# Causal window attention and soft experts: 64-query strips, token-major values with row sums, one VectorE step for bias and maximum

## The chip, the cores and the metric

The kernel runs on one core of one Trainium2 chip. The metric is the device time of one execution in microseconds; a profiled execution gives a span, from the first to the last instruction, and the trace behind the lines below. The five engines are TensorE (PE, with PEld for its weight loads), VectorE (DVE), ScalarE (ACT), GpSimd (POOL) and SyncE (SP, which issues most DMAs).

## The reference

Attention with a causal window of 128 keys and a linear bias by distance, over 8 batches, 8 heads, 576 tokens, 64 features a head; then a mixture of soft experts (8 experts with 4 slots each, so 32 slots) over all 4608 tokens:

```python
scores = q @ k.T / sqrt(64) - slope[h] * abs(i - j)   # only 0 <= i - j < 128
attn = softmax(scores) ; x = attn @ v                 # (B, H, S, D)
x = x.transpose(0, 2, 1, 3).reshape(4608, 512)
logits = x @ phi                                      # (4608, 32)
d = softmax(logits, over tokens) ; c = softmax(logits, over slots)
slot_in = d.T @ x                                     # (32, 512)
slot_out[e] = relu(slot_in[e] @ w1[e]) @ w2[e]        # 512 -> 1024 -> 512
return c @ slot_out                                   # (4608, 512)
```

All of it is in float32.

## The kernel before, in words

**Attention loop.** A batch has five query tiles: four of 128 queries and a tail of 64. A full tile is done in two groups of four heads; the tail is one group of eight heads. This makes 9 groups a batch and 72 in all. A group always holds 4 x 128 columns of scores on 128 partitions (queries on the partitions). The order on each engine is written out by hand (`manual_schedule`), and the loop over `i` walks the groups in a pipeline: group i gets its softmax, group i-3 is transposed, group i-4 meets the values, group i+1 gets its scores.

One group's steps, with the lines of the profile:

- `scores`: TensorE first writes the distance bias into PSUM (bf16 products of `ones` and `ramp`, L248, or L236 for a batch's first tile) and adds the products of 32-query strips with 160 keys (L255, L241). Two halves of the array's rows (two heads) and four column groups (four strips) work at once.
- `merge` (VectorE, L270; L268 and L272 in first and tail tiles): the window of a query covers 128 of the columns held; a predicated copy folds the two triangles into one 128 x 128 square.
- `rowmax` (L290) and `bias` (L293, maximum times the scale), VectorE.
- `expo` (ScalarE, L342): four exponentials of 128 columns, each with its row sum read out (ACTIVATION_READ_ACCUMULATOR).
- `total` (POOL, L298), `inverse` (L302) and `normalise` (L307, four multiplications), VectorE: the probabilities are divided by the row sum.
- `flip` (L352): four transposes; `split`: a copy to SBUF by ScalarE (L359) and two `affine_select` by POOL (L361, L363) that take the folded square apart into the keys of this tile and of the one before.
- `values` (L388): per head, v is the stationary operand (64 columns) and 128 queries stream; x comes out with the features on the partitions. `x_store` (L404, ScalarE) copies it, `x_flip` (L409) and `x_keep` (L418) make the token-major copy.

**Slots, once a batch.** `logits` (L427) for the tiles of the batch, a running maximum and sum over the tokens, transposes, `slot_sum` (L510) and `slot_add` (L523) with rescaling, and the softmax over the slots (L534 to L547) in gaps of VectorE (`fillers`).

**Weights.** w1 and w2 make 64 units of 512 KB. `load_weights_at` spreads the first `NW` = 36 over the loop; 11 more go into buffers that attention has no more use for (`place`), the last 17 into ring buffers that the experts free.

**End.** After the loop stands a hand-written chain for the last groups. Then the experts: `hidden` (L911), `expert_out` (L947), `slot_stack`, `combine` (L968, L974) in the order of `TAIL_ORDER`; `turn` transposes the combine weights.

Of the kernel before, what the change touches and what calls it, by code (L numbers as in the profile page):

```python
# [25 lines left out]
NT = 5  # L26
# [5 lines left out]
NTT = 36  # L32
UW = 1024
NW = 36
KB = 32
WIN = P + KB
NB = S // KB
HW = 512
CW = P + TAIL + NS
WARM = 6  # L40
WEND = 66
W0 = 10
EAGER = 2
FLAG = 3
LAG = 4
FINAL = (3, 4, 0)
# [6 lines left out]
TAIL_ORDER = '''s0 b0v b1a b2v e1n e13 k0 e12 c00 e15 c01 e16 s1 c02 e2n e24 k1 e22 c10 e25 c11 e25 s2 c12 e3n e34 k2 e32 c20 e35 c21 e35 s3 c22 k3 c30 c31 c32'''  # L53
# [3 lines left out]
def width(t):  # L57
    return P if t < 4 else TAIL
# [10 lines left out]
def tile_attn_softmoe(  # L69
# [4 lines left out]
    vd: bass.AP,  # L74
    phid: bass.AP,
    w1d: bass.AP,
    w2d: bass.AP,
    slopes: bass.AP,
# [11 lines left out]
    mask_u = cst[:, 0:P].bitcast(I32)  # L90
    mask_t = cst[:, P:P + TAIL].bitcast(I32)
    delta = cst[:, P + TAIL:]
    pick, sel = cst[:, 0:P], cst[:, P:P + 2 * NS]
    unit_r = cpool.tile([P, P], F32R, name="unit_r")
    ident = unit_r.bitcast(F32)
    fine = cpool.tile([P, 14], F32, name="fine")
    low, m_run, s_run = fine[:, 0:1], fine[:, 1:3], fine[:, 3:4]
    comb = cpool.tile([P, NS], F32, name="comb")
    mix = cpool.tile([P, NS], F32, name="mix")
# [4 lines left out]
    kq = cpool.tile([P, 3 * UW], F32, name="kq")  # L104
    ramp = cpool.tile([P, 2, 2, WIN], BF16, name="ramp")
    ones = cpool.tile([P, P], BF16, name="ones")
    area = cpool.tile([P, 19, HW], F32, name="area")

    kall = kq[:, 0:NB * P].rearrange("p (n j w) -> p n j w", n=NB, j=NPAIR)
    qs = [kq[:, NB * P + 2 * P * i:NB * P + 2 * P * i + 2 * P] for i in range(3)]  # L110
    half = [slice(64 * par, 64 * par + 64) for par in range(2)]

    def halves(i):
        return area[:, i].rearrange("p (u w) -> p u w", u=4)

    xts = [halves(i) for i in (0, 1, 12, 13)]
    xt_t = halves(17)
    p4s = [halves(i) for i in (2, 3, 18)]
    pas, pps = [halves(i) for i in (6, 8, 7)], [halves(i) for i in (7, 9)]
    vs = [area[:, i] for i in (11, 5, 10)]  # L120
    xns = [area[:, i] for i in (16, 4, 14, 15)]
# [3 lines left out]
    areas = {i: area[:, i:i + 2].rearrange("p a w -> p (a w)") for i in range(0, 18, 2)}  # L125
    place = [ks[1], areas[14], ks[0], ks[2]] + [areas[i] for i in (0, 10, 6, 4, 16, 12, 8)]
# [3 lines left out]
    def load_weight():  # L130
# [12 lines left out]
    def order(b):  # L143
        return (1, 2, 3, 4, 0) if b == last else range(NT)

    def pos(b, t):
        return order(b).index(t)

    def lane(b, t):
        return (t - 1) % 4 if b == last else t  # L150

    groups = [(b, t, g) for b in range(B) for t in order(b) for g in range(2 if t < 4 else 1)]
    number = {key: i for i, key in enumerate(groups)}
    n = len(groups)
    v_loads = [(b, t) for b in range(B) for t in range(NT)]
    fin = slice(3 * NS, P)
# [7 lines left out]
    def load_q(i, eng=None):  # L164
        b, t, g = groups[i]
        o = 4 * P * t + 2 * P * g
        (eng or nc.sync).dma_start(qs[i % 3], qd[b, :, o:o + 2 * P])

    def load_k(b, t, eng=None):
        o, e = 4 * P * t, min(4 * P * (t + 1), NB * P)  # L170
        (eng or nc.sync).dma_start(kq[:, o:e], kd[b, :, o:e])

    v_slot = {}

    def load_v(again=False):
        if again:
            b, t, v_slot[last, 0] = last, 0, area[:, 13]
        else:
            b, t = v_loads[len(v_taken)]
            v_slot[b, t] = vs[len(v_taken) % 3]  # L180
            v_taken.append((b, t))
        nc.sync.dma_start(v_slot[b, t][0:width(t)], vd[b, P * t:P * t + width(t)])

    def load_v_pair():
        new = [len(v_taken), len(v_taken) + 1]
        for i in new:
            v_slot[v_loads[i]] = vs[i % 3]
            v_taken.append(v_loads[i])
        for o in (0, DM // 2):
            for i in new:  # L190
                b, t = v_loads[i]
                nc.sync.dma_start(
                    v_slot[b, t][:, o:o + DM // 2], vd[b, P * t:P * t + P, o:o + DM // 2])

    v_taken = []

    with tc.manual_schedule(engines=ORDERED):
        warm = area[:, 2].bitcast(BF16)[:, 0:512]
        nc.vector.memset(warm, 0.0)
        nc.vector.memset(low, LOW)  # L200
        nc.vector.memset(ramp, 0.0)
        nc.vector.memset(ones, 1.0)
        nc.vector.memset(fine[:, 10:11], -1.0)
        nc.gpsimd.memset(cst[:, 0:P], 1.0)
        nc.gpsimd.affine_select(cst[:, 0:P], cst[:, 0:P], [[1, P]], ALU.is_gt, 0.0, base=0, channel_multiplier=-1)
        load_k(0, 0)
        load_q(0, nc.scalar)
        for par in range(2):
            nc.sync.dma_start(ramp[64 * par:64 * par + 1], slopes[par:par + 1])
        load_q(1, nc.scalar)  # L210
        load_q(2, nc.scalar)
        load_k(0, 1)
        tiny = work.tile([P, 1], F32, tag="nm", name="tiny")
# [3 lines left out]
        nc.gpsimd.memset(lg, LOW)  # L217
        nc.gpsimd.memset(area[:, 3, 0:P], 1.0)
        nc.gpsimd.affine_select(
            unit_r, area[:, 3, 0:P], [[1, P]], ALU.is_equal, 0.0, base=0, channel_multiplier=-1)  # L220
        load_v()
        nc.scalar.dma_start(cst[:, P:], cstd)
        nc.scalar.dma_start(phi, phid)
        for t in range(2, NT):
            load_k(0, t)

    def scores(i):
        b, t, g = groups[i]
        s4 = s4s[i % 2]
        parts = [s4[:, 0:2], s4[:, 2:4]]  # L230
        if i == 0:
            parts = [ps_1.tile([P, 2, 2 * P], F32, tag=tag, name="s4_0") for tag in ("pt", "xp")]
        qt = qs[i % 3].rearrange("p (j w) -> p j w", w=width(t))
        if t == 0:
            for par, rows in enumerate(half):
                nc.tensor.matmul(  # L236
                    parts[par][:, :, 0:P], lhsT=ones[rows], rhs=ramp[rows, g, :, 0:P],
                    start=True, stop=False)
            for jj in range(2):
                for par, rows in enumerate(half):  # L240
                    nc.tensor.matmul(  # L241
                        parts[par][:, jj, 0:P], lhsT=qt[rows, jj], rhs=kall[rows, 0:4, 2 * g + jj],
                        start=False, stop=(jj == 1))
        else:
            strips = [(c // 2, c % 2) if t == 4 else (g, c) for c in range(4)]
            for par, rows in enumerate(half):
                for c, (h, r) in enumerate(strips):
                    nc.tensor.matmul(  # L248
# [848 lines left out]
```

## Time and profile before

| what | value |
|---|---|
| time, median of 3 runs | 290.92 us (289.94 to 291.21) |
| span of the profiled execution | 289.1 us; of its time outside the span nothing is recorded |
| busy PE / DVE / ACT / POOL | 272.9 / 233.3 / 204.5 / 92.7 us |
| mean granted TensorE clock | 0.980 |
| last scores of the loop begin | 216.28 us |
| the experts' first product begins | 235.74 us |
| DMA | 72.58 MB, mean 251 GB/s |

Busy time is the union of an engine's records. A TensorE record is a latency (270 to 300 ns for a product), and records overlap, so a busy TensorE may still take more work; the distance between starts tells what one product costs. DMA share is the mean busy share of the core's 16 DMA engines. A group's line in the page gives the line of code, the engine, what is written and read, the count, then busy time, the mean of one, and the idle time before it with what ended it.

### The profile page before, as it was taken

What the parts mean: (1) busy time and instruction counts of PE and PEld (TensorE: products, weight loads), DVE (VectorE), ACT (ScalarE), POOL (GpSimd) and SP (SyncE); (2) the same over time, 40 slices, a digit from 0 to 9 for tenths busy, and PEclk for the clock granted to TensorE, in tenths of its full rate; (3) what the DMA queues carried; (4) which work ended last, traced back from release to release, by engine and by line L of the source; (5) the groups of instructions that cost most, each with busy time, mean ns of one, the idle gap of its engine ahead of it and who ended that gap; (6) DMA issues with size and microseconds to landing.
All of it is one profiled execution on the core that took longest, in us unless ns stands there. A gap on an engine that the chain in (4) does not pass through costs nothing.

```text
span 289.1 us, 13085 instructions
## 1 busy us (share of the span) xinstructions
PE 272.9 (94%) x5164; PEld 191.0 (66%) x5164; DVE 233.3 (81%) x729; ACT 204.5 (71%) x811; POOL 92.7 (32%) x206
## 2 busy tenths in 40 slices
PE   7499999999999999999999999999899999999983
PEld 3367777777677767776777677767676753476641
DVE  3899999999989999988999999979989443234452
ACT  2788888978988978978798887978797241023351
POOL 2025515442444354235324550634455001000000
PEclk9799999999999999999999999999999999999995
DMA  6645278868786887867678869675547789999897
GB/s 193 223 131 169 81 228 266 261 201 284 212 265 201 287 279 242 246 231 247 216 249 258 282 199 291 218 252 173 185 158 238 231 285 311 417 417 398 352 378 285
DMA packets 35025, 72.58 MB, mean 251 GB/s; under 512 B 4210, under 2 KB 15124, under 8 KB 34964
## 3 DMA queue, kind: packets, MB, share of 16 engines
q1 hardware_dynamic: 34244, 71.24, 74.0%
q8 instruction: 41, 0.67, 0.9%
q10 hardware_dynamic: 720, 0.51, 0.6%
q14 instruction: 20, 0.16, 0.1%
HBM read 62.29 MB, written 9.44 MB: 248 GB/s over the span
## 4 chain that ended last, share of the span: by engine, by line
PE 47%; DVE 44%; ACT 3%; issue 3%; POOL 1%; ACTq 0%; DVEq 0%; POOLq 0%
DVE area L307 16%; DVE s L290 11%; PE xp L388 8%; DVE s L270 6%; PE op L947 5%; PE hp L911 5%; PE po L968 4%; PE pt L352 4%; PE s L255 4%; DVE s L268 3%; PE xq L409 2%; PE lp L427 2%; ACT area L342 2%; PE s L248 2%; PE ap L510 1%
## 5 line engine op out<-in xcount | busy, mean ns | idle before, releaser
L342 ACT ACTIVATE area<-s,nb 128x128 f32<-128x128 f32 x288 | 102.5, 374 | 21.5 <-DVE nb L293 20.2
L307 DVE TENSOR_SCALAR area<-area,rs 128x128 f32<-128x128 f32 x286 | 79.2, 338 | 0.6 <-DVE nb L293 0.3
L388 PE MATMUL xp<-area 128*64 128x128 f32 (+1 forms) x1104 | 75.2, 271 | 2.2 <-POOL area L361 1.3
L388 PEld LDWEIGHTS xp<-area 128*64 128x64 f32 x1104 | 56.2, 136 | 17.4 <-issue 8.7
L342 ACT ACTIVATION_READ_ACCUMULATOR area<-s,nb 128x1 f32 x288 | 60.8, 211 | 0.0
L290 DVE TENSOR_REDUCE s<-s 128x4 f32<-128x512 f32 x71 | 49.5, 698 | 2.2
L359 ACT COPY area<-pt 128x512 f32<-128x512 f32 x70 | 42.0, 600 | 11.0 <-PE pt L352 10.8
L298 POOL TENSOR_SCALAR rs<-sm 128x4 f32<-128x4 f32 x70 | 13.8, 197 | 99.7 <-ACT area L342 98.9
L352 PE MATMUL pt<-unit_r,area 128*128 128x128 f32 x284 | 45.6, 282 | 0.0
L255 PE MATMUL s<-kq 64*32 64x160 f32 x1792 | 42.0, 302 | 0.3 <-DMA kq<-k_t 0.3
L352 PEld LDWEIGHTS pt<-unit_r,area 128*128 128x128 f32 x284 | 31.9, 142 | 14.2 <-PE s L255 5.0
L361 POOL TENSOR_SCALAR_AFFINE_SELECT area<-area 128x512 f32<-128x512 f32 x48 | 31.6, 658 | 25.8 <-ACT area L359 24.5
L270 DVE COPY_PREDICATED s<-cst,s 128x512 f32<-128x512 int32 x48 | 32.9, 686 | 0.7 <-PE s L255 0.5
L363 POOL TENSOR_SCALAR_AFFINE_SELECT area<-area 128x512 f32<-128x512 f32 x48 | 31.4, 655 | 3.3
L255 PEld LDWEIGHTS s<-kq 64*32 64x32 f32 x1792 | 29.6, 107 | 1.0 <-DMA kq<-q_t 0.5
L248 PE MATMUL s<-ramp,ones 64*32 64x320 bf16 x448 | 18.7, 310 | 5.0 <-ACT area L342 4.8
L974 DVE COPY ob<-po 128x384 f32<-128x384 f32 x24 | 12.5, 554 | 13.5 <-PE po L968 11.8
L409 PE MATMUL xq<-unit_r,area 128*128 128x128 f32 x136 | 22.0, 284 | 0.5
L404 ACT COPY area<-xp 128x512 f32<-128x512 f32 (+1 forms) x37 | 20.9, 565 | 2.0 <-PE xp L388 1.6
L418 ACT COPY area<-xq 128x512 f32<-128x512 f32 x34 | 20.8, 611 | 0.0
L974 ACT COPY ob<-po 128x384 f32<-128x384 f32 x24 | 10.5, 482 | 13.7 <-PE po L968 13.7
L409 PEld LDWEIGHTS xq<-unit_r,area 128*128 128x128 f32 x136 | 14.5, 141 | 6.4 <-issue 3.2
(167 smaller groups left out, 309.8 us busy)
## 6 DMA issues: line engine op xcount, KB each, us to landing
w<-w SPq DMA_DIRECT2D x53, 512.0 KB, 5.1
out<-ob SPq DMA_DIRECT2D x24, 384.0 KB, 4.2
kq<-q_t SPq DMA_DIRECT2D x69, 128.0 KB, 3.2
kq<-k_t SPq DMA_DIRECT2D x32, 256.0 KB, 3.7
area<-v_n SPq DMA_DIRECT2D x31, 256.0 KB, 4.3
area<-w SPq DMA_DIRECT2D x8, 512.0 KB, 5.0
area<-v_n SPq DMA_DIRECT2D x12, 128.0 KB, 3.4
kq<-w SPq DMA_DIRECT2D x3, 512.0 KB, 6.3
```

What stands on the lines that cost most here:

```text
L248: nc.tensor.matmul(s4[32 * c:32 * c + 32, 2 * par:2 * par + 2, 32 * r:32 * r + WIN], lhsT=ones[rows, 0:32], rhs=ramp[rows, h], start=True, ...
L255: nc.tensor.matmul(s4[32 * c:32 * c + 32, 2 * par + jj, 32 * r:32 * r + WIN], lhsT=qt[rows, 2 * h + jj if t == 4 else jj, 32 * r:32 * r + 32],
L270: nc.vector.copy_predicated(s4[:, :, P:2 * P], bc(mask_u, 1, 4), s4[:, :, 0:P])
L290: nc.vector.tensor_reduce(st[key]["mx"][:, us], merged(key, us), axis=AX.X, op=ALU.max, negate=True)
L307: mul(p4[:, u], p4[:, u], st[key]["rs"][:, u:u + 1])
L342: nc.scalar.activation(s["p4"][:, u], merged(key, u), AF.Exp, bias=s["nb"][:, u:u + 1], scale=SCALE, accum_out=s["sm"][:, u:u + 1],)
L352: nc.tensor.transpose(s["pt"][:, u], s["p4"][:, u], ident)
L359: copy(pa[:, us], s["pt"][:, us])
L361: nc.gpsimd.affine_select(pp[:, us], pa[:, us], [[0, m], [-1, P]], ALU.is_gt, 0.0, base=0, channel_multiplier=1)
L363: nc.gpsimd.affine_select(pa[:, us], pa[:, us], [[0, m], [1, P]], ALU.is_ge, 0.0, base=0, channel_multiplier=-1)
L388: nc.tensor.matmul(xp[D * par:D * par + D, j, 0:w], lhsT=v_slot[b, t - 1 + ph][0:rows, D * h:D * h + D], rhs=src[:, 2 * par + i] if t < 4 ...
L409: nc.tensor.transpose(xq[:, P * j:P * j + P], x_of(b, t)[:, j], ident)
```

## The change: what it does

- **Strips.** A tile is now 128 queries (or the tails of two batches together) in two strips `g` of 64 queries. A strip holds 64 queries of two heads on the 128 partitions and four such pairs in its columns, all eight heads. Each sees 192 keys. There are 36 tiles (`tiles`) instead of 72 groups; keys are loaded in blocks of 64 (`KB`), q 512 columns at a time.
- **Bias and maximum.** The bias is no more a product, except in tile 0, where the same products write the mask. One `tensor_tensor_reduce` for each 128 columns adds a constant `bias` tile to the merged scores, scales by -1/8, writes the result to SBUF (`sq`) and takes the minimum as the exponential's bias. The merge is half as wide (64 columns of each 128).
- **Row sums.** v gets two more columns (`VD` = 66), the first of ones, so that the values product gives the row sums; the exponentials have no accumulator. `values` now has the probabilities as the stationary operand (64 queries) and 66 columns of v streaming, so x comes out token-major; `values_ex` adds the corner (64 keys of the tile before or after) on 64 rows of the array. `x_store` divides by the row sum on VectorE and is token-major; `x_flip`/`x_keep` make the feature-major copy.
- **POOL.** The corner selects are eight a tile, on 64 partitions and 256 columns each.
- **Slots by four tiles.** Logits, maxima and sums run per quad of tiles (`NQ` = 9), with the last quad in the end; the lanes are joined by `lane_rows`, `lane_exp`, `lane_sum`.
- **Loads.** `NW` = 34 ring buffers for weights and 15 placed units; a weight load waits for a one-column memset of POOL (`gated`). v for tails and the last key blocks of even batches are loaded separately.
- **Ends.** The end of the loop is written anew; three of the four transposes of combine weights move there (`turn((0, 1, 2), ...)` and so on) and out of `TAIL_ORDER`.

The core of the diff:

```diff
-NW = 36
-KB = 32
+NW = 34
+KB = 64
...
-        for par, rows in enumerate(half):
-            for c, (h, r) in enumerate(strips):
-                nc.tensor.matmul(
-                    s4[32 * c:32 * c + 32, 2 * par:2 * par + 2, 32 * r:32 * r + WIN],
-                    lhsT=ones[rows, 0:32], rhs=ramp[rows, h], start=True, stop=False)
+        if t == 0:
+            for par, rows in enumerate(half):
+                for c in range(2):
+                    nc.tensor.matmul(
+                        parts[par][half[c], :, 0:WIN], lhsT=slope[rows, c],
+                        rhs=steps[rows, g], start=True, stop=False)
+        for jh in range(2):
+            for par, rows in enumerate(half):
+                for c in range(2):
...
+                    nc.tensor.matmul(
+                        parts[par][half[c], jh, KB * o:WIN], lhsT=qt[rows, j],
+                        rhs=keys, start=(t > 0 and jh == 0), stop=(jh == 1))
...
+    def merge(k, g, us=ALL):
+        nc.vector.copy_predicated(
+            window(k, g, us, 0, KB), bc(mask_le, 1, len(range(4)[us])), window(k, g, us, P, KB))
+    def rowmax(k, g, us=ALL):
...
+        for u in range(4)[us]:
+            nc.vector.tensor_tensor_reduce(
+                out=s["sq"][:, u], in0=window(k, g, u, 0, P),
+                in1=bias[:, u] if tiles[k][1] else zero.to_broadcast([P, P]),
+                scale=-SCALE, scalar=-LOW, op0=ALU.add, op1=ALU.min, accum_out=s["nb"][:, u:u + 1])
...
+            nc.scalar.activation(
+                dst, s["sq"][:, u].rearrange("p (a w) -> p a w", a=2), AF.Exp,
+                bias=s["nb"][:, u:u + 1], scale=-1.0)
...
+    def split(k, g):
...
+        for par in range(2):
+            rows = half[corner(k, g, par)]
+            pa, ex = pas[k % 2][rows, g, par], pps[k % 2][rows, g]
+            for dst, old in ((ex, not early(k, g)), (pa, early(k, g))):
+                if old:
+                    nc.gpsimd.affine_select(
+                        dst, pa, [[0, NPAIR], [-1, KB]], ALU.is_gt, 0.0, base=0, channel_multiplier=1)
...
+    def values(k, to=None):
...
+        for j in range(NPAIR):
+            for par in range(2):
+                for g in range(2):
...
+                    nc.tensor.matmul(
+                        x[par][half[g], j], lhsT=pas[k % 2][:, g, par, j], rhs=v[:, par, j],
+                        start=(j == 0), stop=(t == 0 and j == NPAIR - 1))
+    def values_ex(k):
...
+                    rows = half[corner(k, g, par)]
+                    v = (v4_even, v4_odd)[g] if t == 4 else v_slot[b, t - g]
+                    nc.tensor.matmul(
+                        x[par][half[g], j], lhsT=pps[k % 2][rows, g, j], rhs=v[rows, par, j],
+                        start=False, stop=(j == NPAIR - 1))
+    def x_store(k, pars=(0, 1)):
...
+        for par in pars:
+            nc.vector.tensor_scalar_add(rs[:, par], xp[par][:, :, D], EPS)
+        nc.vector.reciprocal(rs[:, pars[0]:pars[-1] + 1], rs[:, pars[0]:pars[-1] + 1])
+        for par in pars:
+            nc.vector.tensor_tensor(x[:, par], xp[par][:, :, 0:D], bc(rs[:, par], 2, D), op=ALU.mult)
...
+    def load_weight(gated=False):
...
+        if gated:
+            nc.gpsimd.memset(wt[units[n]][:, 0:1], 0.0)
...
+        for k in range(n):                  # the loop, first turns and extras left out
+            merge(k, 0); rowmax(k, 0); merge(k, 1); rowmax(k, 1)      # VectorE
+            filler() x 4
+            flip(k - 1, 0, "a"); flip(k - 1, 1, "b")                  # TensorE
+            values(k - 2); x_flip(k - 3); token_flips(q)
+            take(k - 1, 0); split(k - 1, 0); take(k - 1, 1); split(k - 1, 1)
+            expo(k, 0); token_keep(q); expo(k, 1)                     # ScalarE
+            values_ex(k - 2); logits(q) or slot_sum(q); x_keep(k - 3)
+            scores(k + 1, 0); scores(k + 1, 1); loads(k + 1)
+            x_store(k - 2); token_max(q) or slot_add(q)
```

The last block is the loop in short, with `take` the copy out of PSUM by ScalarE.

More of the change, by code (lines that the diff above doesn't have):

```diff
@@ L116, in tile_attn_softmoe @@
[L116 to L121, printed above, removed]
+    kq = cpool.tile([P, KC + 2 * DM], F32, name="kq")
+    kt = cpool.tile([P, 6 * P], F32, name="kt")
+    ramp = cpool.tile([P, RW], BF16, name="ramp")
+    slope = ramp[:, 0:2 * KB].rearrange("p (c w) -> p c w", c=2)
@@ L412, in xn_of, with chain @@
-    def xn_of(b, t):
-        if b == last and t not in (1, 2):
-            return area[:, {3: 8, 4: 2, 0: 9}[t]]
-        return xns[lane(b, t)] if t < 4 else xns[3]
-    def x_keep(b, t, copy=nc.scalar.copy):
-        copy(xn_of(b, t), st.pop(("xq", b, t)))
-    def lanes(b):
-        return 4 if b < last else 2
-    def logits(b):
-        lp = ps_1.tile([P, 512], F32, tag="mi", name="lp")
-        for j in range(NPAIR):
-            for c in range(lanes(b)):
+    def chain(k, g):
+        merge(k, g)
+        rowmax(k, g)
@@ L600, in join @@
-    def join():
-        st["join"] = ps_1.tile([P, 512], F32, tag="pt", name="join")
-        nc.tensor.matmul(st["join"][fin], lhsT=comb, rhs=acc, start=True, stop=True)
-    def join_keep():
-        nc.scalar.copy(sums[fin], st["join"][fin])
-    lf = free[2]
-    sums = area[:, 3]
-    def logits_last(c):
-        src = x_of(last, FINAL[c])
-        for j in range(NPAIR):
-            nc.tensor.matmul(
-                lf[fin, P * c:P * c + P], lhsT=phi[:, j], rhs=src[:, j], start=(j == 0), stop=(j == NPAIR - 1))
@@ new lines, in tile_attn_softmoe, with spin @@
+            run("act", k)
+            run("dve", k)
+            run("late", k)
+        ka, kb, kc = n - 3, n - 2, n - 1
+        lp = free[3]
+        idle = inp.bitcast(BF16)[:, 0:512]
+        def spin(m):
+            if "spin" not in st:
+                st["spin"] = bank("o", [P, 512], "spin")
+            for _ in range(m):
+                nc.tensor.matmul(st["spin"], lhsT=idle[:, 0:P], rhs=idle, start=True, stop=True)
+        for _ in range(3):
+            load_weight()
+        nc.gpsimd.memset(inp, 0.0)
@@ new lines, in tile_attn_softmoe @@
+        flip(kc, 0, "a")
+        flip(kc, 1, "b")
+        take(kc, 0, nc.scalar.copy)
+        take(kc, 1, nc.vector.tensor_copy)
+        drain()
+        values(kb)
+        values_ex(kb)
+        x_flip(ka)
+        x_keep(ka)
+        run("act", n)
+        for _ in range(5):
+            load_weight()
+        values(kc, [x.rearrange("p (j d) -> p j d", d=P)[:, :, 0:VD] for x in (free[0], free[2])])
+        for _ in range(2):
+            load_weight()
+        x_store(kb)
+        x_flip(kb, bank("b", [P, DM], "xq"))
@@ L882, in tile_attn_softmoe @@
+        turn((6, 7), "a", free[0])
+        for part in range(2):
+            slot_inputs(part)
+            inputs_keep(part)
+        assert not todo and loaded[0] == NW + len(place), (todo, loaded, len(place))
     HC = max(MW)
```

1017 lines of the change are left out of this document (421 added, 596 removed).

## The prediction

> **What bounds the kernel now.** I read the page first: the busy shares and the costliest groups. Its columns in a group are: line, engine, operation, what it writes and reads, count, then busy microseconds, mean ns of one, and idle time before.
>
> ```profile
> span 289.1 us, 13085 instructions
> PE 272.9 (94%) x5164; PEld 191.0 (66%) x5164; DVE 233.3 (81%) x729; ACT 204.5 (71%) x811; POOL 92.7 (32%) x206
> L342 ACT ACTIVATE area<-s,nb 128x128 f32<-128x128 f32 x288 | 102.5, 374 | 21.5 <-DVE nb L293 20.2
> L307 DVE TENSOR_SCALAR area<-area,rs 128x128 f32<-128x128 f32 x286 | 79.2, 338 | 0.6 <-DVE nb L293 0.3
> L388 PE MATMUL xp<-area 128*64 128x128 f32 (+1 forms) x1104 | 75.2, 271 | 2.2 <-POOL area L361 1.3
> L342 ACT ACTIVATION_READ_ACCUMULATOR area<-s,nb 128x1 f32 x288 | 60.8, 211 | 0.0
> L255 PE MATMUL s<-kq 64*32 64x160 f32 x1792 | 42.0, 302 | 0.3 <-DMA kq<-k_t 0.3
> L361 POOL TENSOR_SCALAR_AFFINE_SELECT area<-area 128x512 f32<-128x512 f32 x48 | 31.6, 658 | 25.8 <-ACT area L359 24.5
> ```
>
> Then the busy time by stretches: one batch of nine groups in the middle, and most of the expert stage. The columns are the stretch, its length, busy PE, PEld, DVE, ACT, POOL with their counts, granted clock, DMA share, GB/s.
>
> ```profile
> 95.00:122.60 27.60, 27.07 (x596) 20.02 (x596) 27.20 (x89) 24.32 (x102) 11.02 (x24) 1.00 0.82 262
> 252.00:280.00 28.00, 26.84 (x585) 17.56 (x581) 12.46 (x27) 9.68 (x25) 0.00 (x0) 1.00 0.97 388
> ```
>
> In the attention stage VectorE works 27.20 of 27.60 us per batch: it sets the pace there. TensorE shows 27.07, but its records are latencies that overlap, so its real need has to come from start times. In the expert stage VectorE has half its time free, and TensorE and the DMAs are full; the change hardly touches that stage. So I priced one turn of the attention loop on both engines, from the timeline. VectorE, one undisturbed group (start, duration, instruction):
>
> ```profile
> 118.18 0.68 DVE L270 COPY_PREDICATED s<-cst,s 128x512 f32<-128x512 int32 x1
> 118.89 0.70 DVE L290 TENSOR_REDUCE s<-s 128x4 f32<-128x512 f32 x1
> 119.50 0.17 DVE L302 RECIPROCAL rs<-rs 128x4 f32<-128x4 f32 x1
> 119.63 0.16 DVE L293 TENSOR_SCALAR nb<-s 128x4 f32<-128x4 f32 x1
> 119.78 0.87 DVE L307 TENSOR_SCALAR area<-area,rs 128x128 f32<-128x128 f32 x4
> 120.57 0.69 DVE L270 COPY_PREDICATED s<-cst,s 128x512 f32<-128x512 int32 x1
> ```
>
> Start to start: merge 0.71, maximum 0.61, small steps 0.13 and 0.15, four normalisations 0.79; the group takes 2.39. Nine of them are 21.5 us. The four normalisations take 0.87 here, against a mean of 79.2/71.5 = 1.11 over the run, so some 0.24 x 9 = 2.1 us a batch are lost when they are disturbed. The rest, 27.2 - 21.5 - 2.1 = 3.6 us, is the work per batch of the slot softmax.
>
> TensorE, start to start, from two neighbouring groups, one place with 64-column products (and the group that gives the duration of one), and the end of the loop:
>
> ```profile
> 95.99 1.08 PE L427 MATMUL lp<-area,phi 128*32 128x128 f32 x32
> 97.00 0.66 PE L352 MATMUL pt<-unit_r,area 128*128 128x128 f32 x4
> 97.59 0.66 PE L388 MATMUL xp<-area 128*64 128x128 f32 x8
> ...
> 99.68 1.09 PE L388 MATMUL xp<-area 128*64 128x128 f32 x16
> 100.70 0.33 PE L248 MATMUL s<-ramp,ones 64*32 64x320 bf16 x8
> 100.85 0.73 PE L255 MATMUL s<-kq 64*32 64x160 f32 x32
> 101.51 0.33 PE L494 MATMUL dp<-unit_r,lg 128*128 128x128 f32 x1
> 101.67 0.60 PE L409 MATMUL xq<-unit_r,area 128*128 128x128 f32 x4
> 102.11 0.60 PE L352 MATMUL pt<-unit_r,area 128*128 128x128 f32 x4
> ```
> ```profile
> 62.85 0.45 PE L388 MATMUL xp<-area 64*64 64x64 f32 x8
> ```
> ```profile
> L388 PE MATMUL xp<-area 64*64 64x64 f32 x112 | 6.3, 230 | 0.4
> ```
> ```profile
> 216.82 1.06 PE L510 MATMUL ap<-area,dn 128*32 128x512 f32 x8
> 217.81 0.66 PE L352 MATMUL pt<-unit_r,area 128*128 128x128 f32 x4
> ```
>
> Four transposes 0.59 (0.44 when more transposes precede), values 1.02, bias products 0.15, scores 0.66, logits 1.01 and slot sum 0.99 once a batch. A whole group is 2.42, and a batch, with its lighter first tile and the x transposes, about 25.7 of the 27.6 us. TensorE is thus close behind VectorE: a change that frees VectorE alone could win 2 us in 27.6. It has to lighten both.
>
> **The change part by part, per new tile** (two strips, the work of two old groups; 36 tiles for 72 groups; two old groups last 2 x 27.6/9 = 6.13 us).
>
> TensorE.
> - Transposes of the probabilities: still eight, now in one run: 0.59 + 0.44 = 1.03.
> - Values: 32 records of 66 columns, two at a time, instead of 2 x 16 of 128. One pair of 128 columns steps by (1.09 - 0.27)/7 = 0.117, so 66 columns would step by 0.060; the row at 62.85, four pairs of 64 columns, gives (0.45 - 0.23)/3 = 0.073 with the first pair's start-up in it. I take 0.065, nearer the low end because only the first pair pays the start: 16 x 0.065 + 0.10 for the change of array shape (1.02 against 8 x 0.117 = 0.94 shows 0.08) = 1.14.
> - Corner products, new and on 64 rows: 32 records, four at a time if the two row halves run beside each other as the scores do: 8 x 0.065 + 0.10 = 0.62.
> - Scores: eight sets of four with 192 columns. The row at 100.85 gives (0.73 - 0.30)/3 = 0.143 for 160, so 0.172 for 192: 1.48 for both strips. The bias products go (they stay only in tile 0).
> - x transposes 0.59. Slot work per four tiles 1.01 + 0.99 + 0.3 = 2.3, so 0.58 a tile.
>
> Sum 1.03 + 1.14 + 0.62 + 1.48 + 0.59 + 0.58 = 5.44. Tile 0 has no corner and shorter scores (2 x 0.18 bias, four sets of 64 and four of 128 columns, 1.19 in all): 4.53. Seven and two of them in nine tiles: **5.24 us a tile**.
>
> VectorE. Removed: normalisations, reciprocals, bias steps and totals. Half-width merges, and the step that joins bias and maximum, have these nearest rows:
>
> ```profile
> 103.33 0.29 DVE L535 TENSOR_TENSOR ln<-dp,cm 128x128 f32<-128x128 f32 x1
> 103.54 0.69 DVE L270 COPY_PREDICATED s<-cst,s 128x512 f32<-128x512 int32 x1
> ...
> 106.11 0.73 DVE L523 SCALAR_TENSOR_TENSOR acc<-acc,al,ap 128x512 f32<-128x512 f32 x1
> 106.77 0.41 DVE L272 COPY_PREDICATED s<-cst,s 128x256 f32<-128x256 int32 x1
> 107.22 0.70 DVE L290 TENSOR_REDUCE s<-s 128x4 f32<-128x512 f32 x1
> ```
> ```profile
> 96.00 0.37 ACT L342 ACTIVATE area<-s,nb 128x128 f32<-128x128 f32 x1
> 96.27 0.19 ACT L342 ACTIVATION_READ_ACCUMULATOR area<-s,nb 128x1 f32 x1
> 96.36 0.36 ACT L342 ACTIVATE area<-s,nb 128x128 f32<-128x128 f32 x1
> ```
>
> - Merges: 2 x 0.45 = 0.90.
> - The joint step, eight a tile, is not in this trace; call its start-to-start price x. Low end 0.21: a plain two-operand step of the same size from PSUM (103.33 to 103.54). High end 0.38: its whole duration, 0.29, and then an accumulator read-out as ScalarE pays it (96.27 to 96.36, 0.09). I take 0.28, nearer the low end, because the four steps of a strip do not depend on each other; the 0.07 on top is most of a read-out. The Trainium skill, "VectorE: DVE Perf Modes", section "Two Vector instructions with no wait between them", says that a VectorE operation that also writes its accumulator is two instructions, and no VectorE row here shows one. With ScalarE's 0.09 for the second, the step would be 0.30, and without a second instruction 0.21.
> - Storing x moves here from ScalarE and now divides by the row sums: two additions and a reciprocal 0.13 + 0.15 + 0.15, two products of 256 elements at 0.35 (between 0.21 for 128 and 0.66 for 512, 106.11 to 106.77): 1.13.
> - Slot softmax 3.6 x 9/36 = 0.9 less the fewer columns: 0.83.
>
> Sum 2.86 + 8x: **5.10 us a tile** (4.54 to 5.90). The disturbance of the normalisations goes with them.
>
> ScalarE is busy 204.5/36 = 5.7 us for the work of a tile now. The read-outs (60.8 us in all, partly beside the next exponential) and the x store go; eight exponentials at 0.27 (96.00 to 96.27) are 2.2 us against 2.9 with the read-out (96.00 to 96.36), so it stays at or under 5.0, hidden beside 5.2; the operand from SBUF instead of PSUM I cost at nothing, as long as that margin covers it. POOL: eight half-size selects of 64 partitions at less than 0.66 each, 2.6 to 5.3 us; their results are wanted one tile later, so they cost nothing unless near the high end. The one-column memsets that pace the weight loads stand behind these selects, and SP waits for them with the loads of v, q and k behind it; these buffers are wanted one to two tiles (5 to 10 us) later, so that too costs nothing. If this cover fails, the scores wait for q.
>
> **The sum.** Two engines need 5.24 and 5.10; today the busiest reaches 98%. Two alike and coupled will do worse: I take 5.24/0.96 = 5.45. The first scores start 0.3 later (a larger constant load), say 5.5. The first three turns have no values or x behind them and are set by VectorE's merges and maxima, 0.90 + 8 x 0.28 = 3.1, and some waiting: 10.5 together. Then 32 turns: 5.5 + 10.5 + 32 x 5.45 = 190.4, against 216.8 today.
>
> ```profile
> 235.74 7.16 PE L911 MATMUL hp<-w,acc 128*32 128x512 f32 x64
> ```
>
> From the last scores to the experts' first product it is 235.7 - 216.8 = 18.9 us today. The new end has one more TensorE turn without scores (5.44 - 1.48 = 4.0), 1.03 + 1.14 + 0.62 + 0.59 + 1.14 = 4.5 for the last transposes and values, then a serial chain of stores, flips, logits, maximum, exponential, slot sum and inputs, which I put at 11.5 from today's end, where the like chain fills most of 18.9: 20. The three transposes of the combine weights leave the last stage for this chain's gaps; that stage stays at 289.1 - 235.7 = 53.4 less 1. The DMAs allow that: after the last scores 30 weight units of 512 KB and 24 outputs of 384 KB are to be moved, 25.2 MB, at the 388 GB/s of the expert stage 65 us, against 72 here; they would bind only from a span of 255 down. Span: 190.4 + 20 + 52.4 = 263. The span before is 289.1 and the median of the runs 290.92, so 1.8 lie around it: 265; I round up for unknown waits and predict **266 us**. What a measurement of this kernel can tell from no change is about 0.5%, 1.5 us.
>
> **Rivals.**
> - *Corner products two at a time.* In the corner step both row halves of the array write the same bank. No row here has that: the scores put their row halves in two banks. If the halves take turns, it is 16 x 0.065 instead of 8, +0.52 for 28 tiles: 5.24 becomes 5.64, the turn 5.87, and the time 279. For it: the scores were kept apart. Against: the halves go to different partitions. The Trainium skill, "TensorEngine Tiling (Array Packing)", section "Restrictions and Gotchas", says that different row tiles cannot access one PSUM bank at the same time; by it this rival would be the outcome.
> - *VectorE sets the pace.* With x of 0.32 to 0.38 it needs 5.4 to 5.9, turns of 5.6 to 6.1: 271 to 289. The top of it is no change.
> - *Slower, by the same place.* If the joint step waits out its own 0.29 and then a small instruction of 0.17 (the reciprocal's duration), x is 0.45, VectorE needs 6.5, the turn is 6.6, and the time 305. The point from which this decides is x = 0.40, where the turn is 6.2 and the time 290. For it: ScalarE's exponentials with a read-out step by 0.36 for 128 elements. Against: nothing on VectorE here waits out a full duration without a dependence.
> - *The chains couple better*, 98% and a shorter end: 252.
>
> **How the numbers follow.** Forecast 0.60 (255 to 273), better 0.05, corner products in turn 0.13, VectorE's pace 0.12, slower 0.10. The range 254 to 284 holds the forecast, the corner rival and the lower half of VectorE's: 0.8. Faster: 0.60 + 0.05 + 0.13 + 0.09 = 0.87; same 0.03; slower 0.10.
>
> **What would show it.** Turns of 5.3 to 5.6 us in the loop; joint steps 0.25 to 0.31 apart; corner products starting in fours; no read-outs on ScalarE in the loop; the experts' first product near 210 and the last stage of 52 to 53. Wrong would be: VectorE idle at the scores while TensorE is full beyond 5.6 (a product price missed), joint steps beyond 0.4, or TensorE waiting for q or for POOL's selects.

## The result, and the profile after

The changed kernel takes 262.4 us (median of 4 runs, 261.6 to 264.6) against 291.1 us for the kernel before on the same chip: a ratio of 0.902, 95% interval 0.897 to 0.907. A second set of runs gave 0.901 (0.896 to 0.905). Medians are over all runs of a kernel; ratios and intervals leave out runs more than 1.5% above its fastest. The span of the profiled execution went from 289.1 to 262.9 us.

From the page of the kernel after: the span, the busy shares, the shares of the chain that ended last, and the groups that answer to those shown of before.

```profile
span 262.9 us, 12396 instructions
PE 240.9 (92%) x4863; PEld 177.9 (68%) x4864; DVE 178.4 (68%) x979; ACT 167.5 (64%) x483; POOL 98.5 (37%) x269
PE 67%; DVE 15%; ACT 7%; issue 4%; DMA 3%; POOL 1%; DVEq 0%; ACTq 0%; POOLq 0%
L290 ACT ACTIVATE area<-sq,nb 128x128 f32<-128x128 f32 x288 | 89.8, 398 | 5.2 <-PE pt L308 3.2
L275 DVE CUSTOM_DVE_ANT_0 sq<-s,cst 128x128 f32<-128x128 f32 x224 | 52.0, 287 | 7.1 <-ACT area L311 0.5
L275 DVE DVE_READ_ACCUMULATOR2_ANT nb<- 128x1 f32 x288 | 23.8, 83 | 0.1
```

VectorE lost 55 us of work and ScalarE 37 (233.3 and 204.5 before). The chain now runs on TensorE for two thirds of the span. By stretches (columns as in the prediction), the same 27.6 us in the loop as before, and a longer piece of the loop:

```profile
95.00:122.60 27.60, 25.25 (x570) 20.00 (x566) 22.47 (x131) 21.17 (x63) 13.70 (x38) 1.00 0.85 272
```
```profile
40.00:180.00 140.00, 135.63 (x2986) 107.48 (x2985) 113.88 (x665) 110.92 (x326) 72.56 (x197) 1.00 0.82 263
```

VectorE is busy 113.88 of 140 us; it was 27.20 of 27.60. A turn is the time from the transposes of one tile to those of the next. One turn from the timeline (start, duration), TensorE first, then VectorE and ScalarE:

```profile
125.95 1.09 PE L308 MATMUL pt<-unit_r,area 128*128 128x128 f32 x8
126.97 1.15 PE L340 MATMUL xp<-va,area 128*64 128x66 f32 x32
128.05 0.66 PE L372 MATMUL xq<-unit_r,xs 128*128 128x128 f32 x4
128.64 0.70 PE L352 MATMUL xp<-va,area 64*64 64x66 f32 x32
129.27 1.08 PE L385 MATMUL lp<-xs,phi 128*32 128x128 f32 x32
```
```profile
126.39 0.42 DVE L266 COPY_PREDICATED s<-cst,s 128x256 f32<-128x256 int32 x1
126.95 0.29 DVE L275 CUSTOM_DVE_ANT_0 sq<-s,cst 128x128 f32<-128x128 f32 x1
127.17 0.08 DVE L275 DVE_READ_ACCUMULATOR2_ANT nb<- 128x1 f32 x1
127.17 0.28 DVE L275 CUSTOM_DVE_ANT_0 sq<-s,cst 128x128 f32<-128x128 f32 x1
127.38 0.08 DVE L275 DVE_READ_ACCUMULATOR2_ANT nb<- 128x1 f32 x1
...
127.66 2.46 ACT L290 ACTIVATE area<-sq,nb 128x128 f32<-128x128 f32 x8
```

TensorE's stages follow each other without a gap: transposes 1.02, values 1.08, x transposes 0.59, corner products 0.63 in front of the logits (0.52 in front of the scores). A turn without slot work I call plain; it lasts 4.63 to 4.79 us. The joint step is two records, but the read-out starts together with the next step, so the steps are 0.21 apart.

### The profile page after: what moved, and what is told of

It reads as the page before. It is cut to its first block, busy times and chain, and to the rows that moved or that the text cites. A ratio compares the mean times of both kernels' runs of the same rounds, so it can differ in the third digit from the quotient of the medians.

```text
span 262.9 us, 12396 instructions
## 1 busy us (share of the span) xinstructions
PE 240.9 (92%) x4863; PEld 177.9 (68%) x4864; DVE 178.4 (68%) x979; ACT 167.5 (64%) x483; POOL 98.5 (37%) x269
## 4 chain that ended last, share of the span: by engine, by line
PE 67%; DVE 15%; ACT 7%; issue 4%; DMA 3%; POOL 1%; DVEq 0%; ACTq 0%; POOLq 0%
PE s L252 11%; PE pt L308 10%; PE xp L340 10%; PE op L777 6%; DVE sq L275 6%; PE xq L372 6%; PE hp L741 5%; PE xp L352 5%; PE po L798 4%; ACT area L290 3%; PE ap L439 3%; DMA kq<-q_t 3%; PE lp L385 3%; DVE xs L366 3%; DVE s L266 2%
## 5 line engine op out<-in xcount | busy, mean ns | idle before, releaser
L290 ACT ACTIVATE area<-sq,nb 128x128 f32<-128x128 f32 x288 | 89.8, 398 | 5.2 <-PE pt L308 3.2
L327 POOL TENSOR_SCALAR_AFFINE_SELECT area<-area 64x256 f32<-64x256 f32 x112 | 46.5, 416 | 89.4 <-ACT area L311 83.8
L275 DVE CUSTOM_DVE_ANT_0 sq<-s,cst 128x128 f32<-128x128 f32 x224 | 52.0, 287 | 7.1 <-ACT area L311 0.5
L252 PE MATMUL s<-kq 64*64 64x192 f32 (+2 forms) x1088 | 51.4, 318 | 5.4 <-DMA kq<-q_t 2.0
L324 POOL TENSOR_SCALAR_AFFINE_SELECT area<-area 64x256 f32<-64x256 f32 x112 | 46.2, 413 | 7.5
L252 PEld LDWEIGHTS s<-kq 64*64 64x64 f32 x1088 | 38.9, 139 | 14.0 <-issue 4.9
L340 PE MATMUL xp<-va,area 128*64 128x66 f32 x1120 | 41.3, 225 | 1.0 <-POOL w L149 0.5
L340 PEld LDWEIGHTS xp<-va,area 128*64 128x64 f32 x1120 | 36.0, 137 | 7.2 <-issue 5.4
L266 DVE COPY_PREDICATED s<-cst,s 128x256 f32<-128x256 int32 (+1 forms) x73 | 30.6, 419 | 8.4 <-PE s L252 8.4
L366 DVE TENSOR_TENSOR xs<-xp,rs 128x256 f32<-128x256 f32 x70 | 26.5, 420 | 6.9 <-PE ap L439 5.9
L372 PE MATMUL xq<-unit_r,xs 128*128 128x128 f32 x144 | 23.8, 287 | 0.7 <-DVE rs L363 0.3
```

What stands on the lines that cost most here:

```text
L252: nc.tensor.matmul(parts[par][half[c], jh, KB * o:WIN], lhsT=qt[rows, j], rhs=keys, start=(t > 0 and jh == 0), stop=(jh == 1))
L266: nc.vector.copy_predicated(window(k, g, us, 0, KB), bc(mask_le, 1, len(range(4)[us])), window(k, g, us, P, KB))
L275: nc.vector.tensor_tensor_reduce(out=s["sq"][:, u], in0=window(k, g, u, 0, P), in1=bias[:, u] if tiles[k][1] else zero.to_broadcast([P, P] ...
L290: nc.scalar.activation(dst, s["sq"][:, u].rearrange("p (a w) -> p a w", a=2), AF.Exp, bias=s["nb"][:, u:u + 1], scale=-1.0)
L324: nc.gpsimd.affine_select(dst, pa, [[0, NPAIR], [-1, KB]], ALU.is_gt, 0.0, base=0, channel_multiplier=1)
L327: nc.gpsimd.affine_select(dst, pa, [[0, NPAIR], [1, KB]], ALU.is_ge, 0.0, base=0, channel_multiplier=-1)
```

## The experiments

Times are medians beside the kernel before, which took 290.7 to 291.8 us in the same sets of runs. A difference to the changed kernel is the difference of the two ratios (0.901 for the changed kernel) times 291 us; with the intervals of two ratios it is known to about 2 us. A mean turn is the mean of the 31 turns from the fourth tile's transposes to the 35th's in a profiled execution; it is 5.36 us in the first profile of the changed kernel and 5.28 in the second.

| kernel | us | ratio, 95% interval | against its parent |
|---|---|---|---|
| before, no normalisations | 288.0 | 0.987 (0.982 to 0.993) | -3.8 us |
| before, no bias products | 290.0 | 0.996 (0.993 to 1.000) | -1.1 us |
| before, neither | 281.7 | 0.968 (0.963 to 0.972) | -9.4 us |
| after, 2 joint steps more | 270.0 | 0.926 (0.922 to 0.930) | +7 us |
| after, 8 joint steps more | 300.8 | 1.034 (1.030 to 1.038) | +39 us |
| after, corner products in pairs | 268.1 | 0.921 (0.918 to 0.924) | +6 us |
| after, read-outs of the sums | 278.2 | 0.957 (0.954 to 0.961) | +16 us |
| after, bias by products | 272.2 | 0.928 (0.920 to 0.936) | +8 us |
| after, other start order | 261.1 | 0.888 (0.882 to 0.894) | -4 us |
| after, light weights in the loop | 265.4 | 0.910 (0.906 to 0.914) | +3 us |
| after, once more | 263.6 | 0.901 (0.896 to 0.905) | |

**What bounded the kernel before.** Three kernels take the two suspects away, one by one and together.

```diff
     def normalise(key, us, mul=nc.vector.tensor_scalar_mul):
         p4 = st[key]["p4"]
-        for u in range(4)[us]:
-            mul(p4[:, u], p4[:, u], st[key]["rs"][:, u:u + 1])
+        return
```

> The kernel before without its four multiplications by the reciprocal of the row sum in each group (the probabilities stay unnormalised). Leaves VectorE about 20.4 us of work per batch of nine groups where it had 27.2, and TensorE its 25.7. Theory (both engines close to the bound before): TensorE sets the pace at once, the loop gives 8 x (27.6 - 26) = some 13 us, so about 277 us (271 to 281). Rival (VectorE alone was the limit): 72 groups x 0.79 us = 57 us less, about 234 us.

```diff
-            for par, rows in enumerate(half):
-                for c, (h, r) in enumerate(strips):
-                    nc.tensor.matmul(
-                        s4[32 * c:32 * c + 32, 2 * par:2 * par + 2, 32 * r:32 * r + WIN],
-                        lhsT=ones[rows, 0:32], rhs=ramp[rows, h], start=True, stop=False)
...
-                            rhs=kall[rows, m0:m0 + 5, 2 * h + jj], start=False, stop=(jj == 1))
+                            rhs=kall[rows, m0:m0 + 5, 2 * h + jj], start=(jj == 0), stop=(jj == 1))
```

> The kernel before without the bias products of TensorE in all groups that are not the first of a batch (the distance bias is left out there). TensorE loses about 0.15 us in each of 56 groups. Theory (VectorE sets the pace before): 0 to -2 us, about 290 us. Rival (TensorE sets the pace): 56 x 0.15 = 8 us less, about 282 us.

Both edits together:

> The kernel before without the normalisations and without the bias products (both are left out of the result). Theory (TensorE is next behind VectorE): 25.7 - 1.2 = 24.5 us of TensorE per batch, the loop gives about 22 us, more than the two alone together: about 269 us (263 to 273). Rival (TensorE not close behind): the same as without the normalisations alone.

Measured: -3.8, -1.1 and -9.4 us. The signs and the order are those of the theory, and VectorE alone was not the limit; but the two larger gains are less than half of what I expected. The kernel without normalisations says why: its loop stretch (40 to 180 us), the same stretch of before, and its chain.

```profile
40.00:180.00 140.00, 140.00 (x2912) 104.35 (x2904) 91.49 (x246) 123.16 (x509) 56.37 (x124) 1.00 0.80 254
```
```profile
40.00:180.00 140.00, 138.14 (x2816) 101.87 (x2814) 133.77 (x427) 120.32 (x497) 55.57 (x121) 1.00 0.79 249
```
```profile
PE 90%; DVE 2%; ACT 2%; issue 2%; DMA 1%; POOL 1%; ACTq 0%; DVEq 0%; POOLq 0%
```

With VectorE busy 91.5 of 140 us, TensorE has no gap at all and its chain is 90% of the span. From the transposes at 27.52 us to those 63 groups later at 216.43 a group lasts 3.00 us, 27.0 a batch. So TensorE needed 27.0 of the 27.6 us before, not my 25.7. One thing I left out stands in its timeline: the values of a batch's last tile are 32 records that last 116.11 - 114.44 = 1.67, where I counted 1.02 for every group.

```profile
113.86 0.66 PE L351 MATMUL pt<-unit_r,area 128*128 128x128 f32 x4
114.44 1.74 PE L387 MATMUL xp<-area 128*64 128x64 f32 x32
116.11 0.33 PE L248 MATMUL s<-ramp,ones 64*32 64x320 bf16 x8
```

The single transposes of the token statistics, some four a batch at 0.16 us each (L494, 101.51 to 101.67 in the rows of the prediction), were not in my sum either; 0.65 + 4 x 0.16 is about the 1.3 that it lacked. With both edits the loop goes to 2.92 a group, 26.3 a batch, and the scores and what went with them take 98.04 - 97.33 = 0.71 us:

```profile
97.33 0.77 PE L250 MATMUL s<-kq 64*32 64x160 f32 x32
98.04 0.33 PE L488 MATMUL dp<-unit_r,lg 128*128 128x128 f32 x1
```

Scores and bias products took 101.51 - 100.70 = 0.81 before (rows of the prediction). So the bias products cost 0.10 and not 0.15; 56 times that is the 5.6 us by which the kernel without both is faster than the one without normalisations alone, where the same edit alone had brought 1.1. VectorE and TensorE were at their limit together, and only a change that lightens both could win much.

**VectorE's room after the change.** More joint steps, whose results are written twice:

```diff
-        for u in range(4)[us]:
+        extra = [2, 3] if k and g == 1 else []
+        for u in list(range(4)[us]) + extra:
```

> The changed kernel with two of the joint bias-and-maximum steps of the second group done twice in each turn: +0.42 us of VectorE per turn (two steps at 0.21 us). Theory (TensorE sets the pace, VectorE has about 0.8 us of slack per turn): 0 to +2 us, 262 to 264 us. Rival (VectorE sets the pace): 35 x 0.42 = +15 us, 277 us.

```diff
-        for u in range(4)[us]:
+        for u in list(range(4)[us]) * (2 if k else 1):
```

> The changed kernel with all eight joint steps of a turn done twice: +1.7 us of VectorE per turn, 4.5 becomes 6.2 where TensorE has 5.2. Theory: the slack is used up and VectorE sets the pace, 35 x (6.25 - 5.3) = +30 us, about 293 us (285 to 300): this is what the joint step at 0.42 us would have cost. Rival (VectorE set the pace already): 35 x 1.7 = +60 us, 322 us.

Two more steps cost 7 us, half of their work: neither theory. In its profiled run half of the plain turns stayed at 4.7 us and half grew to between 4.9 and 5.1; of the turns with slot work some grew from 6.0 to 6.5. The mean turn is 5.45 us against 5.36 and 5.28; that locates 3 to 5 us of the 7 (this profiled run, 267.9 us, is also 2 us faster than the median of its kernel). Eight more cost 39 us, above the theory's 30 and far below 60. There VectorE is the chain, and its mean turn is 6.38 us:

```profile
DVE 55%; PE 26%; ACT 11%; issue 4%; DMA 3%; ACTq 0%; DVEq 0%
```

Sixteen steps at 0.211 are 3.4, so VectorE's other work is 3.0 a turn (I had 2.86), and with eight steps it needs 4.7 of the turn's 5.3. This run is also about what the kernel would be if a joint step took 0.42: slower than before. The rival that I put at 0.40 and more was the right danger; the step just isn't that dear.

**The corner products.** They are sorted by row half, so that only two can run at once:

```diff
-        for j in range(NPAIR if t else 0):
-            for par in range(2):
-                for g in range(2):
-                    rows = half[corner(k, g, par)]
...
+        for r in range(2):
+            for j in range(NPAIR if t else 0):
+                for par in range(2):
+                    for g in range(2):
+                        if corner(k, g, par) != r:
+                            continue
+                        rows = half[r]
...
```

> The changed kernel with the corner products (32 per turn) ordered by row half, first all of the one half of the key rows and then all of the other, so that two products at a time can run beside each other and not four. The result is the same. Theory (products of both row halves run four at a time although they write one bank, and TensorE sets the pace): the stage of 0.52 us becomes about 1.0 us, in 28 turns +0.5 us each: +14 us, about 276 us. Rival 1 (row halves that write one bank are run one after the other anyway): 0. Rival 2 (TensorE isn't the bound): under +4 us.

Measured +6 us. The stage, in front of the logits as in the turn shown above (0.63):

```profile
129.98 0.98 PE L355 MATMUL xp<-va,area 64*64 64x66 f32 x32
130.89 0.32 PE L388 MATMUL lp<-xs,phi 128*32 128x128 f32 x4
```

It lasts 0.91, 0.28 more, and 28 x 0.28 = 8 us. The starts tell how. Each row below begins with the first product of the stage, and the next one takes in more of them: 8 and 16 in the changed kernel, 4 and 8 in the sorted one.

```profile
128.64 0.35 PE L352 MATMUL xp<-va,area 64*64 64x66 f32 x8
128.64 0.46 PE L352 MATMUL xp<-va,area 64*64 64x66 f32 x16
```
```profile
129.98 0.33 PE L355 MATMUL xp<-va,area 64*64 64x66 f32 x4
129.98 0.45 PE L355 MATMUL xp<-va,area 64*64 64x66 f32 x8
```

In the changed kernel two more fours take (0.46 - 0.35)/2 = 0.06 us each; sorted, two more pairs take (0.45 - 0.33)/2 = 0.06 each. A four costs no more than a pair, so in the changed kernel four products do run beside each other, two of each row half, although in 24 of the 28 tiles both halves write the same bank. In the other four, the tails of two batches, they write two banks, and the stage is just as long (0.63 in this one):

```profile
106.20 0.70 PE L352 MATMUL xp<-va,area 64*64 64x66 f32 x32
106.83 1.08 PE L385 MATMUL lp<-xs,phi 128*32 128x128 f32 x32
```

My +14 was too much because the edit didn't keep the halves apart: the second half's first product starts at 130.28, 0.30 us after the first half's, while that one still has three pairs to start. With no overlap at all the stage would be longer by some 8 x 0.06 = 0.5 (an estimate), as I had it. The Trainium skill, "TensorEngine Tiling (Array Packing)", section "Restrictions and Gotchas", says that different row tiles cannot access one PSUM bank at the same time. For these products, whose results go to different partitions of the bank, the trace disagrees: starts and stage are the same with one bank and with two.

**ScalarE.** The exponentials read their row sums out again, into a tile that nobody uses:

```diff
-                bias=s["nb"][:, u:u + 1], scale=-1.0)
+                bias=s["nb"][:, u:u + 1], scale=-1.0, accum_out=s["sm"][:, u:u + 1])
```

> The changed kernel with the row sums read out again by ScalarE's exponentials (accum_out into a tile that nobody uses). Eight exponentials at 0.343 us instead of 0.31 and the read-outs: ScalarE goes from about 4.2 to 4.5 - 5.0 us per turn, still below the turn of 5.36 us. Theory (read-outs fall into ScalarE's slack): 0 to +5 us, 262 to 267 us. Rival (ScalarE lies on the path between VectorE's maxima and TensorE's transposes in each turn): 35 x 0.3 to 0.8 = +10 to +28 us.

Measured +16 us: the rival. The chain, and ScalarE's turn with TensorE's next transposes:

```profile
ACT 52%; PE 35%; issue 4%; DVE 3%; DMA 3%; POOL 1%; ACTq 0%; POOLq 0%; DVEq 0%
```
```profile
122.72 1.07 ACT L313 COPY area<-pt 128x512 f32<-128x512 f32 x2 [1.19 <-PE pt L310]
123.68 0.42 ACT L292 ACTIVATE area<-sq,nb 128x128 f32<-128x128 f32 x1
123.98 0.20 ACT L292 ACTIVATION_READ_ACCUMULATOR area<-sq,nb 128x1 f32 x1
124.08 0.40 ACT L292 ACTIVATE area<-sq,nb 128x128 f32<-128x128 f32 x1
...
126.39 0.39 ACT L292 ACTIVATE area<-sq,nb 128x128 f32<-128x128 f32 x1
...
126.78 0.56 ACT L377 COPY xs<-xq 128x512 f32<-128x512 f32 x1
```
```profile
127.39 0.88 PE L310 MATMUL pt<-unit_r,area 128*128 128x128 f32 x6 [0.98 <-ACT xs L377]
```

ScalarE is not full here, it waits 1.19 us at the start of the turn. But it sits in a ring with TensorE: the transposes of the probabilities use the same bank as the x transposes, so they wait for ScalarE to take these (0.98 us of waiting), ScalarE takes those only behind its exponentials, and its next turn starts with a copy that waits for the transposes. With read-outs the exponentials step by (126.39 - 123.68)/7 = 0.39 us; without, by (2.46 - 0.40)/7 = 0.29 (eight last 2.46 us in the row above, one 0.40). Eight of them make the ring 0.75 longer, and the plain turns went from 4.69 to 5.42.

So the ring has no slack in a plain turn of the changed kernel. One of them, in order of time:

```profile
121.26 1.09 PE L308 MATMUL pt<-unit_r,area 128*128 128x128 f32 x8 [0.24 <-ACT xs L375]
122.01 1.07 ACT L311 COPY area<-pt 128x512 f32<-128x512 f32 x2 [0.59 <-PE pt L308]
122.97 2.46 ACT L290 ACTIVATE area<-sq,nb 128x128 f32<-128x128 f32 x8
125.32 0.58 ACT L375 COPY xs<-xq 128x512 f32<-128x512 f32 x1
```

The copy ends at 125.90, the next transposes start at 125.95 (above): 4.69 us. TensorE's own products fill the same 4.69 without a visible gap, so a plain turn stands on two limits at once, TensorE and this ring; the prediction had no ring. The turn before, from 116.63 to 121.26, has the shorter scores of a batch's first tile, 0.38 us less for TensorE, and still lasts 4.63: TensorE waits for ScalarE's copy (0.24 us by the first row). I had compared ScalarE's busy time with the turn; the ring was the measure.

**The bias.** It is added by TensorE's products in every tile, as in tile 0, and the joint step adds zeros:

```diff
-        if t == 0:
-            for par, rows in enumerate(half):
-                for c in range(2):
-                    nc.tensor.matmul(
-                        parts[par][half[c], :, 0:WIN], lhsT=slope[rows, c],
-                        rhs=steps[rows, g], start=True, stop=False)
+        for par, rows in enumerate(half):
+            for c in range(2):
+                nc.tensor.matmul(
+                    parts[par][half[c], :, 0:WIN], lhsT=slope[rows, c],
+                    rhs=steps[rows, g if t == 0 else 2], start=True, stop=False)
...
-                in1=bias[:, u] if tiles[k][1] else zero.to_broadcast([P, P]),
+                in1=zero.to_broadcast([P, P]),
```

> The changed kernel with the distance bias added by TensorE's products in every tile, as in tile 0, and a column of zeros as the second operand of the joint step. The result is the same; one constant load of 256 KB less. Theory (TensorE sets the pace): two runs of bias products at 0.16 us in each of 28 turns, 28 x 0.32 = +9 us, about 271 us. Rival (the pace is set by VectorE or by waits between the engines): 0 to +2 us.

Measured +8 us (the difference is known to 3 us here), and a mean turn of 5.59 against 5.28 in the profiled run beside it: +0.31. One turn of 7.4 us in it holds a stall (below); the plain turns went from 4.68 to 4.95. TensorE pays nearly in full, as it does where it sets the pace:

```profile
125.80 0.34 PE L236 MATMUL s<-ramp 64*64 64x384 bf16 x4
125.96 0.83 PE L249 MATMUL s<-kq 64*64 64x192 f32 x16
...
```

**Transfers.** The first loads in another order, and the loop's weight loads made small:

```diff
         load_k(0, 1)
-        load_q(1)
         nc.scalar.dma_start(cst[:, 0:KB + NS], cstd[:, 0:KB + NS])
         load_q(0, nc.scalar, slice(1, 2))
+        load_q(1, nc.scalar)
         nc.scalar.dma_start(cst[:, KB + NS:], cstd[:, KB + NS:])
...
-        load_v()
-        nc.scalar.dma_start(phi, phid)
-        nc.scalar.dma_start(ends, seld)
-        for t in range(2, 4):
-            load_k(0, t)
+        load_k(0, 2)
...
+        if k == 0:
+            load_v()
+            load_k(0, 3)
         if k < 3:
             load_v()
+        if k == 3:
+            nc.sync.dma_start(phi, phid)
+        if k == 4:
+            nc.sync.dma_start(ends, seld)
```

> The changed kernel with its first loads in another order: q of the second tile on ScalarE's queue ahead of the bias constants, the first v and the later k after them, phi and the end constants some tiles later. Theory (the first turns wait for q behind loads that are wanted later): the second tile's scores start near 5.5 us and not at 8.4, and 2 to 4 us of it stay at the end: about 259 us. Rival (the transfers as a whole limit the start, in whatever order): within 1 us of the changed kernel.

```diff
         if gated:
-            nc.gpsimd.memset(wt[units[n]][:, 0:1], 0.0)
-        nc.sync.dma_start(wt[units[n]], (w1d, w2d)[m][e, :, UW * k:UW * (k + 1)])
+            nc.gpsimd.memset(wt[units[n]], 0.0)
+        c = 16 if gated else UW
+        nc.sync.dma_start(wt[units[n]][:, 0:c], (w1d, w2d)[m][e, :, UW * k:UW * k + c])
```

> The changed kernel with the 34 weight loads of the attention loop cut to 16 of their 1024 columns (the rest is zero, so most of the expert weights are left out); SP issues as many transfers, 17 MB fewer are moved in the loop. GpSimd fills the whole tiles with zeros, which is some more work for it. Theory A (the stalls of TensorE in the loop, and the late start, are transfers that stand behind the weights): the turns of 6.2 to 7.8 us go, -6 to -10 us in all, about 254 us. Theory B (they are not): 0 to +3 us.

And the changed kernel beside them:

> The changed kernel as it is, beside the others of this call: 0.902 of the time before, about 262.4 us.

The second tile's scores, in the changed kernel and with the other start order:

```profile
8.42 2.84 PE L252 MATMUL s<-kq 64*64 64x192 f32 x32 [2.03 <-DMA kq<-q_t]
```
```profile
7.38 0.88 PE L248 MATMUL s<-kq 64*64 64x192 f32 x16 [1.25 <-DMA kq<-q_t]
```

They start 1.0 us earlier, not 3 (1.6 against the second profile of the changed kernel, where they start at 8.94), and still wait for q; the fourth tile's transposes start at 21.9 us instead of 24.4, and 4 us remain at the end by the ratios (intervals 0.882 to 0.894 against 0.896 to 0.905), 2.5 by the medians of all six runs each. So the order of the first loads is worth about 1%, and this version is faster than both kernels. The weights are not what the loop waits for: with light ones the DMA share falls from 0.85 to 0.59 while the mean turn stays, 5.30 us against 5.28. (Some plain turns last 5.03 instead of 4.68, likely for the fills of GpSimd, so a small gain elsewhere could be hidden.) That kernel's extra 3 us are at its start, where turn 3 takes 8.4 us instead of 6.0; that this comes from GpSimd's fills of whole tiles (0.95 us each) between its selects is likely and was not tried by itself.

```profile
95.00:122.60 27.60, 26.51 (x584) 21.37 (x580) 23.80 (x137) 21.86 (x64) 19.08 (x40) 1.00 0.59 179
```

Two long turns of the changed kernel's first profile, 6.2 us at 24.3 and 7.8 at 102.9, do not recur in its second (5.4 and 5.8). Turns like them stand at other places in other runs: 9.7 us at 149.3 in the sorted kernel, 7.4 at 172.7 in the one with bias products. At 102.9 and in these two TensorE stops for 1.1 to 2.1 us in or before the scores with no wait that the profile names. Their cause stays open.

## Why the prediction was right, point by point

- *Both engines must be lightened*: right, and more so than I said. The step "about 25.7 of the 27.6 us" for TensorE was too low by 1.3. The claim built on it, that freeing VectorE alone could win 2 us in 27.6 (16 in all), measured 3.8 in all.
- *TensorE per tile, 5.24*: too high, by small terms. Values 1.08 for 1.14, corner products 0.52 to 0.63 for 0.62, scores 1.48 for 1.48, transposes 1.02 for 1.03. A plain turn with corner products is 4.69 us. The sum for the mean tile becomes 1.02 + 1.08 + 0.59 + 0.52 + 1.48 + 0.58 = 5.27, less 8/36 of the corner products and of the 0.38 by which tile 0's scores are shorter (189.01 - 187.91 = 1.10, rows below): 5.07, with the slot work as predicted.
- *The turn, 5.45 = 5.24/0.96*: from the end of the first three turns (18.45) to the end of the last scores (189.01) 32 turns take 5.33 each; 5.07/5.33 is 0.95. The two long turns are in this; in the second profile the same turns take 5.26 each, which gives 0.96. The allowance for coupling held, the need was a little smaller. 32 x 0.12 = 3.8 us less than predicted. But the allowance was meant for TensorE and VectorE; a part of what fills it is ScalarE's ring, which I had not foreseen, so that its size fits is partly luck.
- *The first three turns, 5.5 + 10.5 = 16.0*: measured 18.45. I took the first scores as the only ones that wait for a load, and the second tile's wait for q until 8.42. This took back 2.5 of the 3.8 us. It is a wait for q, which the prediction named as a sign of being wrong; it occurs here alone and not in the loop. Turn 3 is slow as well (5.9 us): its value products wait for GpSimd's selects and a memset.

```profile
18.45 1.09 PE L308 MATMUL pt<-unit_r,area 128*128 128x128 f32 x8
19.47 0.33 PE L340 MATMUL xp<-va,area 128*64 128x66 f32 x2
20.20 0.41 PE L340 MATMUL xp<-va,area 128*64 128x66 f32 x4 [0.40 <-POOL area L327]
21.16 1.03 PE L340 MATMUL xp<-va,area 128*64 128x66 f32 x26 [0.55 <-POOL w L149]
```

- *The joint step, x = 0.28*: 0.21, the low end. The term on top, "most of a read-out", was wrong: the read-out (0.08) runs beside the next step. The Trainium skill's rule in "VectorE: DVE Perf Modes", section "Two Vector instructions with no wait between them", that such an operation is two instructions agrees with the trace. The price that I lent it from ScalarE was wrong. VectorE needs 4.7 a turn instead of 5.10, so the rival "VectorE sets the pace" fell by its x.
- *ScalarE "at or under 5.0, hidden"*: the busy time is hidden, but the margin I named was no margin: ScalarE's ring closes at 4.69 us in a plain turn. Its exponentials step by 0.29 and not by my 0.27. With read-outs the ring takes 5.42, and the kernel 16 us more.
- *Corner products two at a time, 279*: did not occur: a four starts every 0.06 us, as a pair does. Its price, 0.52 a tile, was about right for halves that strictly take turns; the sorted kernel, whose halves overlap in part, paid 0.28.
- *The end*: from the last scores to the experts' first product 209.33 - 189.01 = 20.3 us (predicted 20), the last stage 53.5 (predicted 52.4, before 53.4).

```profile
187.91 0.34 PE L239 MATMUL s<-ramp 64*64 64x384 bf16 x4
...
189.01 1.43 PE L385 MATMUL lp<-xs,phi 128*32 128x128 f32 x32
...
209.33 3.19 PE L741 MATMUL hp<-w,inp 128*32 128x512 f32 x25
```

The span, 262.9, met the 263 of the sum because the faster turns (-3.8), the late start (+2.5) and the last stage (+1.1) nearly cancel. That it came so close is luck. The profiled execution took 264.6 us, 1.7 over its span, as I had allowed, but it was the slowest of four, with the two long turns in it, and the median is 262.4. These 2.2 us and my rounding up of 1 make most of the 3.6 by which the 266 was too high.

Where the 29 us come from, by the runs: the loop alone. The last scores end at 189.0 instead of 216.8, and after them nothing is gained. Two parts taken back by themselves cost 16 us (the read-outs) and 8 (the bias products). They are no shares of the 29, since a part taken back can make another engine the limit, as the read-outs do with ScalarE. What the new shape of the strips and the row sums from the values product bring was not tried by itself.

## What to carry to other kernels

Where two engines are both within a few per cent of the turn, taking work off one shows almost nothing (3.8 and 1.1 us here, and 9.4 for both together); price a change on both, and check the price of the second engine by a run that unloads the first, since gapless records tell more than a sum of stages. Measure an engine's margin by the ring of waits it sits in (here: a shared bank between two kinds of transposes) and not by its busy time. And look at the first turns apart: 1% lay in the order of a few loads.

## What the runs showed of the hardware that I had not expected

- VectorE's accumulator read-out is hidden: joint steps of 128 elements with a read-out of 83 ns follow each other at 0.21 us. ScalarE's is not: its exponentials of 128 elements step by 0.39 us with the read-out ((126.39 - 123.68)/7) and by 0.29 without ((2.46 - 0.40)/7).
- Products of 64 rows and 66 columns start every 0.06 us, in pairs of one row half and just so in fours of two row halves that write one bank at different partitions: twice as many products in the same time.
